# RWKV-7 recurrence in chunks, then hash-routed experts: score products in quarters, the old state by diagonal blocks, C in both layouts, and the decay exchange moved to TensorE

## The chip, the cores and the metric

The kernel runs on one core of one Trainium2 chip. The metric is the device time of one execution in microseconds (us), lower is better. One run gives one time; a separate profiled execution gives the trace.

## The reference

Four batches of eight heads, 768 steps, head size 40, all float32. The recurrence is sequential over the steps; its output, with all heads side by side (3072 rows of 320), goes through one of eight experts, chosen by a hash of the token's id.

```python
for t in range(S):                                   # S = 768
    y[:, :, t] = einsum('bhd,bhde->bhe', rt, state)  # state before the step
    Sa = einsum('bhde,bhe->bhd', state, at)
    state = state * wt[:, :, None, :] - einsum('bhd,bhe->bhde', Sa, bt) \
            + einsum('bhd,bhe->bhde', vt, kt)
x = y.transpose(0, 2, 1, 3).reshape(B * S, H * D)
expert = token_ids * 2654435761 % 8
out[expert == e] = maximum(x[expert == e] @ w1[e], 0) @ w2[e]   # (320, 1024), (1024, 320)
```

## The kernel before

**Chunks.** The steps are cut into 12 chunks of 64. A tile is one chunk of two batches, so there are 24 tiles, and two states (`st`, ring of `NG` = 2) that alternate. `u` is the tile's number, `C` = 64, `D` = 40, `R` = 104, `HP` = 4 pairs of heads; `par` tells the head of a pair, `be` the batch. The two heads of a pair lie at columns or partitions 0 to 39 and 64 to 103 (`half40`); 40 to 63 between them are zero. Within a chunk the recurrence becomes matrix products: decayed inputs are formed, a triangular system is inverted, and all steps of the chunk follow from it.

**The order.** Every step is put into `plan` with a tick by `at_tick(tick, step)`, where the tick's fraction is the step's place in `STEPS`. The list is then sorted, and TensorE, VectorE, ScalarE and GpSimd each take their instructions in exactly that order (`manual_schedule`); each waits for what it needs and holds up all that stands behind it. Only SyncE's queue (SP), which issues most loads, is ordered by the framework. One tick is one tile's worth: tile u has its first part at tick u, its second at tick u + `LAG` = u + 8. So ticks 0 to 7 hold first parts alone (the fill), 8 to 23 both, 24 to 31 second parts alone (the drain).

**First part** (`tile_a`). Loads of a, b, k and of the decay products p and q; GpSimd multiplies them to `at` (for a) and `z` (for b and k) at tick u - 0.3; TensorE turns both (`t_ps`, `z_ps`, an identity product each), ScalarE copies them to `at_t` and `z_t`. Step `a` makes the scores `a_ps`: 16 products (`quarters()`: pair, head, batch) of 40 partitions, 128 columns of `z_t` and 64 of `at_t`. Six ScalarE copies take out the diagonal blocks `pk` and the block `no` between them, and VectorE multiplies the rest with the mask `after` into `mk`, straight from PSUM.

**Inversion** (`group_i`). Four tiles at a time, VectorE transposes `pk` to `nb`, does 31 pairs of an outer product (L460) and an addition (L463), and transposes the result to `ut` and `ug`. GpSimd makes `um` from `ug`.

**Second part** (`tile_m`, `tile_s`, `tile_b`). `x_ps` and `u_ps` complete the inverse; `r_ps` is old state by `at_t` (step `r0`, in the tick before) plus `mk` by v (step `r1`); `c_ps` is that by `um`, C's transpose, which ScalarE copies into `x_t`. Step `nc` turns C back by eight transposes into `x`, with two ScalarE copies. Step `rc` makes the read-out scores `rc_ps` from `x_t` and `r_t` (16 products again), VectorE masks them to `mr`. Step `s` adds the old state, by an identity product of all 104 rows and 320 columns for each batch, and 16 products of `z` and `x`; VectorE scales by `pend` into `st`. Step `y` multiplies `r_t` with `sd` (the state turned, step `sd`) and `mr` with `z`; VectorE scales by `py` to `xs`, and two GpSimd DMAs write it to `x_rows`.

**Decay rounds** (`decays`). Six times, for four tiles each, VectorE forms running products of w over quarters of 32 steps (`pb`, `qb`), each step an instruction. The two halves of a chunk lie in different partitions, so the end product of one half is written to HBM and read back for the other (`end_dram`, `ends`). GpSimd scales p (L310) and q (L316) and issues their stores; rounds start five ticks ahead of need.

**Routing and experts.** The routing is cut into steps from tick 8 on, two a tick (`sums_ps` counts tokens; `mine` compares ids with an iota of GpSimd). Eight experts follow, each a gather, 24 + 32 products, and a scatter.

**PSUM.** All the attention's products use one pool of 4 buffers of two banks.

Of the kernel before, what the change touches and what calls it, by code (L numbers as in the profile page):

```python
# [41 lines left out]
def kernel(  # L42
# [74 lines left out]
    psa = apool("psa", 4, space=bass.MemoryType.PSUM)  # L117

# [33 lines left out]
    en_r = ring("en", 2, [BLK, HP, P], all_of)  # L152
# [16 lines left out]
    end_dram = [nc.dram_tensor(f"end{i}", (RN, 3, B * H, D), F32) for i in range(NR)]  # L169

    def psum(name):
        return psa.tile([P, 2, 512], F32, tag="psa", name=name)

    def bank(shape, name):
        n = 1
        for s in shape[1:]:
            n *= s
        t = psum(name)[:, 0, 0:n]
        return t if len(shape) == 2 else t.rearrange("p (x y) -> p x y", x=shape[1])
# [34 lines left out]
    STEPS = ["r1", "at_t", "z0", "c", "z1", "r_t", "nc", "rc", "a", "s", "x", "r0", "y", "v_t", "u", "sd"]  # L214
# [15 lines left out]
    def decays(ri, t0, span, t_ends):  # L230

        x = rounds[ri]
        todo = []

        def step(f):
            todo.append(f)
            return f
# [5 lines left out]
        BH = B * H  # L243

        def store(i, src):
            for y in range(2 * RN):
                nc.gpsimd.dma_start(pq_dram[ri][i][y * HC:(y + 1) * HC].rearrange("t bh e -> bh t e"),
                                    src[y * BH:(y + 1) * BH].rearrange("p (t e) -> p t e", e=D))

        def ends_rows(i):  # L250

            return end_dram[ri][:, i:i + 2].rearrange("n x bh e -> n (x bh) e")

        @step
        def _():
            x["pb"] = pb = work.tile([P, HC * D], F32, tag="pb", name="pb", bufs=1)
            x["qb"] = qb = work.tile([P, (HC + 1) * D], F32, tag="qb", name="qb", bufs=1)
# [3 lines left out]
            nc.sync.dma_start(end_dram[ri][:, 2], ones[0:RN * BH, 0:D])  # L261
# [5 lines left out]
        @step  # L267
        def _():
            nc.vector.memset(segs(x["pb"])[:, :, 0, :], 1.0)


        qs = [x_ for x_ in range(SL - 2, -1, -1)]
        for i in range(1, SL):
            @step
# [3 lines left out]
        for i in qs:  # L278
            @step
# [4 lines left out]
        @step  # L284
        def _():
# [3 lines left out]
            x["ends"] = ends = work.tile([P, SEG + 1, D], F32, tag="ends", name="ends", bufs=1)  # L289
# [6 lines left out]
        @step  # L296
        def _():
            ends = x["ends"]
            nc.vector.tensor_tensor(ends[:, 0:SEG], x["own"][:],
                                    ends[:, SEG].unsqueeze(1).to_broadcast([P, SEG, D]), op=OP.mult)  # L300
            nc.sync.dma_start(ends_rows(0), ends[:, 0])
# [4 lines left out]
        @step  # L306
# [6 lines left out]
        @step  # L313
        def _():
            q = segs(x["qb"])
            nc.gpsimd.tensor_tensor(q, q, x["ends"][:, 1:].unsqueeze(2).to_broadcast([P, SEG, SL, D]),  # L316
                                    op=OP.mult)
            nc.gpsimd.tensor_copy(x["qb"][:, HC * D:], x["ends"][:, SEG])
            store(1, x["qb"][:, D:])

        for i, f in enumerate(todo):
            at_tick(t0 + span * i / len(todo), order=8)(f)

        @at_tick(t_ends)
        def _():

            en = en_r(ri)
            for rn in range(RN):
                nc.sync.dma_start(en[rn * B:(rn + 1) * B].rearrange("b hp (two x) -> b (hp two) x", two=2)[:, :, 0:D],
                                  end_dram[ri][rn, 0].rearrange("(b h) e -> b h e", h=H))  # L330

        @at_tick(t_ends + 1.0)
        def _():
            en = en_r(ri)
            p = bank([P, HP, B * RN], "en_ps")
            for hp in range(HP):
                nc.tensor.transpose(p[0:R, hp, :], en[0:B * RN, hp, 0:R], ident[0:B * RN, 0:B * RN])
            x["pend"] = t = work.tile([P, HP, RN, B], F32, tag="pend", name="pend", bufs=NR)
            nc.scalar.copy(t[0:R].rearrange("p h n b -> p h (n b)"), p[0:R])
# [4 lines left out]
    def tile_a(u):  # L344
# [38 lines left out]
        for i in range(2):  # L383
            @at_tick(u, f"z{i}")
            def _(i=i):
                if i == 0:
                    x["z_t"] = work.tile([P, 2, HP, P], F32, tag="z_t", name="z_t", bufs=1)
                    x["z_ps"] = psum("z_ps")
                p = x["z_ps"][0:R, i, :].rearrange("p (h t) -> p h t", h=HP)
                for hp in range(HP):  # L390
                    nc.tensor.transpose(p[:, hp, :], x["z"][:, i, hp, :], ident[:])  # L391
                nc.scalar.copy(x["z_t"][0:R, i], p)
                if i == 1:
                    x.pop("z_ps")

        @at_tick(u, "a")
        def _():
            gi, ti = divmod(u, GRP)
            p = psum("a_ps")
# [20 lines left out]
            for be in range(2):  # L420
                rows = half(1 - be)
                nc.vector.tensor_tensor(mk[rows], scores(rows, be, 0, C),  # L422
                                        after[rows].unsqueeze(1).unsqueeze(1).to_broadcast([C, 2, HP, C]), op=OP.mult)
# [50 lines left out]
    def hx(p, hp):  # L474

        return p * HP + hp
# [32 lines left out]
    def tile_s(u, t0):  # L509
# [12 lines left out]
        @at_tick(t0 - 1.0)  # L522
# [11 lines left out]
        def _():  # L534

            x["x_t"] = t = work.tile([P, HP, 2 * P], F32, tag="x_t", name="x_t", bufs=1)
            p = psum("v_ps")
# [7 lines left out]
    def tile_b(u, t0):  # L545
# [6 lines left out]
        def _():  # L552
            x["r1_ps"] = p = psum("r1_ps")[:, 0, :]
# [18 lines left out]
        def _():  # L572
            p = psum("c_ps")
            for hp, par, be in quarters():
                rows = (half if par == 0 else half40)(par)
# [401 lines left out]
```

## Time and profile before

| | |
|---|---|
| median of 3 runs | 1059.66 us (1057.06 to 1066.82) |
| profiled execution | 1068.85 us, span 1067.0 us |
| mean granted TensorE clock | 0.851 |
| TensorE busy | 869.2 us, 81% |
| VectorE / ScalarE / GpSimd busy | 407.8 / 241.9 / 317.8 us |
| DMA | 83.26 MB, mean 78 GB/s |
| from the start to the first inner product of the second part (`x_ps`) | 161.75 us |
| first start of `rc_ps`, of tile 1 | 214 us |
| `rc_ps` of tile 1 to that of tile 16 (15 full ticks) | 357 us |
| `rc_ps` of tile 16 to that of tile 22 (6 drain ticks) | 98 us |
| from 686 us on: gather, experts, scatter | 381 us |

Times are counted from the first instruction. A matrix product stands in the trace as two records, a weight load (PEld) beside each; a transpose as one. [...] A busy TensorE is not TensorE at its peak; what tells is the distance from the start of one group to the start of the next. In the square brackets of a timeline stands how long the engine had been idle and what ended it.

### The profile page before, as it was taken

Reading aid. Unit: us, or ns where it says so; the run is one execution under the profiler, and the core shown is the slowest. Engines: PE = TensorE matmul, PEld = TensorE weight load, DVE = VectorE, ACT = ScalarE, POOL = GpSimd, SP = SyncE. Lnnn points to the kernel's source line nnn. Section 1 sums busy time; section 2 is a strip of 40 time slices with the busy share of each in tenths; the row PEclk is TensorE's granted clock in tenths of the full one; section 3 lists DMA queues with packets and bytes.
Section 4 is the critical chain, followed back from the end, with each engine's and each line's share of the span. In section 5 each row is a group of like instructions: output and inputs, shape, how many; then the busy total and the mean of one; then the engine's idle time right before and its main releaser. Section 6 shows DMA issues by size and latency. Waiting matters only on the chain.

```text
span 1067.0 us, 21146 instructions
## 1 busy us (share of the span) xinstructions
PE 869.2 (81%) x8886; PEld 622.3 (58%) x8886; DVE 407.8 (38%) x831; ACT 241.9 (23%) x544; POOL 317.8 (30%) x392
## 2 busy tenths in 40 slices
PE   0128275599899979999999999679999999999994
PEld 0027265488777868887887778525354453544533
DVE  6223797678765774334445721110110101101110
ACT  0014143233334333334333322100100000000000
POOL 3562523622553482322222112031120211201101
PEclk9999998687778866557666976679999999999997
DMA  3744553642454354332112221352241222312000
GB/s 71 159 98 103 111 113 64 137 99 62 97 104 94 64 104 89 67 67 48 30 30 39 52 39 24 111 165 68 75 140 56 88 69 77 136 62 69 19 1 21
DMA packets 164338, 83.26 MB, mean 78 GB/s; under 512 B 140942, under 2 KB 152975, under 8 KB 164240
## 3 DMA queue, kind: packets, MB, share of 16 engines
q1 hardware_dynamic: 154256, 56.95, 23.6%
q0 software_dynamic: 9984, 24.93, 9.5%
q8 instruction: 71, 1.16, 0.5%
q14 instruction: 27, 0.22, 0.1%
HBM read 65.76 MB, written 17.39 MB: 78 GB/s over the span
## 4 chain that ended last, share of the span: by engine, by line
PE 69%; DVE 8%; DMA 6%; ACT 5%; POOL 5%; issue 4%; SPq 3%; POOLq 0%; DVEq 0%; ACTq 0%
PE up_ps L821 18%; PE dn_ps L831 13%; PE s_ps L195 5%; PE a_ps L195 5%; PE rc_ps L195 5%; PE r_ps L195 4%; PE y_ps L195 4%; PE u_ps L195 2%; PE sd_ps L646 2%; PE z_ps L391 2%; PE t_ps L429 2%; PE nc_ps L588 2%; PE x_ps L195 1%; DMA ends<-end 1%; PE c_ps L195 1%
## 5 line engine op out<-in xcount | busy, mean ns | idle before, releaser
L821 PE MATMUL up_ps<-xt,w 128*128 128x512 f32 (+1 forms) x384 | 191.7, 630 | 8.6 <-issue 8.6
L821 PEld LDWEIGHTS up_ps<-xt,w 128*128 128x128 f32 (+1 forms) x384 | 62.7, 189 | 133.4 <-issue 133.4
L831 PE MATMUL dn_ps<-w,ht 128*128 128x320 f32 x512 | 139.9, 434 | 0.0
L831 PEld LDWEIGHTS dn_ps<-w,ht 128*128 128x128 f32 x512 | 96.6, 190 | 45.3 <-issue 6.1
L835 POOL DMA_INDIRECT out_dram<-o,idx_all x32 | 32.0, 999 | 272.0 <-ACT o L834 236.0
L638 POOL DMA_DIRECT2D x_rows<-xs x48 | 28.1, 590 | 268.5 <-DVE xs L635 142.4
L429 PE MATMUL t_ps<-ident,at 128*104 128x128 f32 x96 | 22.7, 380 | 81.8 <-POOL at L374 81.8
L824 DVE TENSOR_SCALAR ht<-up_ps 128x512 f32<-128x512 f32 x32 | 22.1, 692 | 174.6 <-PE up_ps L821 138.8
L463 DVE TENSOR_TENSOR ub<-ub,outer 128x31 f32<-128x31 f32 (+15 forms) x186 | 85.9, 462 | 6.4
L195 PE MATMUL a_ps<-at_t,z_t 40*128 40x64 f32 x768 | 84.8, 388 | 0.4
L460 DVE TENSOR_TENSOR outer<-ub,nb 128x31 f32<-128x31 f32 (+15 forms) x186 | 81.9, 440 | 3.9
L195 PEld LDWEIGHTS a_ps<-at_t,z_t 40*128 40x128 f32 x768 | 80.2, 296 | 4.5 <-issue 2.5
L599 DVE TENSOR_TENSOR mr<-rc_ps,after 128x1024 f32<-128x1024 f32 x24 | 29.3, 1222 | 125.0 <-PE rc_ps L195 125.0
L826 ACT ACTIVATE ht<-up_ps 128x512 f32<-128x512 f32 x32 | 19.1, 597 | 194.9 <-PE up_ps L821 194.9
L429 PEld LDWEIGHTS t_ps<-ident,at 128*104 128x104 f32 x96 | 13.9, 173 | 83.6 <-POOL at L374 82.2
L813 DVE COPY xt<-xg_ps 128x256 f32<-128x256 f32 x32 | 13.2, 412 | 128.2 <-PE xg_ps L811 128.2
L422 DVE TENSOR_TENSOR mk<-a_ps,after 64x512 f32<-64x512 f32 x48 | 33.1, 689 | 73.1 <-ACT no L417 72.6
L195 PE MATMUL rc_ps<-r_t,x_t 40*128 40x64 f32 x768 | 59.4, 313 | 0.8 <-ACT x_t L578 0.7
L195 PEld LDWEIGHTS rc_ps<-r_t,x_t 40*128 40x128 f32 x768 | 55.6, 220 | 4.5 <-ACT x_t L578 1.2
L391 PE MATMUL z_ps<-ident,z 128*104 128x128 f32 x192 | 41.8, 358 | 17.4 <-POOL z L376 7.8
L195 PE MATMUL s_ps<-st,ident 104*104 104x320 f32 x88 | 50.6, 726 | 0.0
L834 ACT COPY o<-dn_ps 128x320 f32<-128x320 f32 x32 | 13.6, 426 | 148.4 <-PE dn_ps L831 148.4
(148 smaller groups left out, 1275.4 us busy)
## 6 DMA issues: line engine op xcount, KB each, us to landing
w<-in_moe_w_dram SPq DMA_DIRECT2D x8, 1280.0 KB
w<-in_moe_w_dram SPq DMA_DIRECT2D x8, 1024.0 KB
ql<-q_rows SPq DMA_DIRECT2D x48, 160.0 KB
pb<-in_w_dram SPq DMA_DIRECT2D x24, 160.0 KB
al<-in_a_dram SPq DMA_DIRECT2D x48, 80.0 KB
kb<-in_b_dram SPq DMA_DIRECT2D x48, 80.0 KB
kb<-in_k_dram SPq DMA_DIRECT2D x48, 80.0 KB
r<-in_r_dram SPq DMA_DIRECT2D x48, 80.0 KB
```

Of the source, the lines that this page charges most:

```text
L195: nc.tensor.matmul(out_, lhsT=lhsT, rhs=rhs, start=start, stop=stop, skip_group_check=True)
L391: nc.tensor.transpose(p[:, hp, :], x["z"][:, i, hp, :], ident[:])
L422: nc.vector.tensor_tensor(mk[rows], scores(rows, be, 0, C), after[rows].unsqueeze(1).unsqueeze(1).to_broadcast([C, 2, HP, C]), op=OP.mult)
L429: nc.tensor.transpose(p[0:R, hp, :], src[:, hp, 0:R], ident[:])
L460: nc.vector.tensor_tensor(tv, ub[:, 0:j + 1, j:j + 1].to_broadcast([P, j + 1, m]), nb[:, j, j + 1:].unsqueeze(1).to_broadcast([P, j + 1, m ...
L463: nc.vector.tensor_tensor(o, o, tv, op=OP.add)
L599: nc.vector.tensor_tensor(t[:].rearrange("p two h t -> p (two h) t"), p[:].rearrange("p two (h t) -> p (two h) t", t=C), after[:].unsqueez ...
L638: nc.gpsimd.dma_start(x_rows[r0:r0 + C, :], xs[half(be), :])
L821: nc.tensor.matmul(p[:], lhsT=w1[0:m, c, f * P:(f + 1) * P], rhs=xt[0:m, c, 0:n], start=(c == 0), stop=(c == 2))
L824: nc.vector.tensor_scalar(ht[:, f, 0:n], p[:], 0.0, None, op0=OP.max)
L831: nc.tensor.matmul(p[:], lhsT=ht[:, f, j * P:(j + 1) * P], rhs=w2[:, f, :], start=(f == 0), stop=(f == FP - 1))
L835: st = nc.gpsimd.indirect_dma_start(out=out[:], out_offset=bass.IndirectOffsetOnAxis(ap=idx, axis=0), in_=o[:], in_offset=None, bounds_che ...
```

## The change

- **PSUM**: 4 buffers of one bank (`psa`, by `bank`) and 2 of two banks (`psb`, by `two_banks`), for z, a, v, c, rc and sd.
- **Scores**: each product of `a_ps` and `rc_ps` is made as two of 64 columns, in the order (half of the columns, head).
- **mk**: two ScalarE copies out of PSUM and one GpSimd product with `after`, in place of two VectorE products.
- **Old state**: four products of 40 columns of the identity with 160 columns of `st`, the two diagonal blocks alone; `st` scaled by two VectorE products of the blocks.
- **C**: `nc_ps` is 16 products of `um` and `r1` beside those of `c_ps`, in place of eight transposes of the copied C; C is copied to `x_t` in two halves.
- **Order**: new `STEPS`; `y` and `sd` at tick t0 + 1; py's load at t0; both z transposes and their copies in one step.
- **Decay rounds**: the end product of the first half goes to the second by a product with the matrix `partner` and an addition of `second`; no `end_dram`. q is scaled by VectorE; SP issues the stores; `pend` comes from one transpose. Rounds 0 and 1 both stand before tick -0.9; the load of a round has a step of its own one tick ahead.
- **Inversion**: its last step at +3.2 ticks, from +3.5.

```diff
-    STEPS = ["r1", "at_t", "z0", "c", "z1", "r_t", "nc", "rc", "a", "s", "x", "r0", "y", "v_t", "u", "sd"]
+    STEPS = ["r1", "at_t", "z", "c", "y", "r_t", "sd", "a", "rc", "x", "s", "v_t", "r0", "u"]
...
     def store(i, src):
             for y in range(2 * RN):
-                nc.gpsimd.dma_start(pq_dram[ri][i][y * HC:(y + 1) * HC]...
+                nc.sync.dma_start(pq_dram[ri][i][y * HC:(y + 1) * HC]...
...
-            nc.sync.dma_start(ends_rows(0), own[:, 0])
-            nc.sync.dma_start(ends[:, SEG], ends_rows(1))
+            p = bank([P, D], "f_ps")
+            nc.tensor.matmul(p, lhsT=partner[:], rhs=own[:, 0], start=True, stop=True)
...
+            nc.vector.tensor_scalar(ends[:, SEG], x.pop("f_ps"), second[:, 0:1], None, op0=OP.add)
...
-            nc.gpsimd.tensor_tensor(q, q, x["ends"][:, 1:].unsqueeze(2).to_broadcast([P, SEG, SL, D]),
+            nc.vector.tensor_tensor(q, q, x["ends"][:, 1:].unsqueeze(2).to_broadcast([P, SEG, SL, D]),
...
-            for hp, par, be in quarters():
-                c0 = (hp * 2 + be) * C
-                mm(p[:, par, c0:c0 + C], x["z_t"][half40(par), be, hp, :], x["at_t"][half40(par), hp, be, :])
+            for hp in range(HP):
+                for be in range(2):
+                    for i in range(2):
+                        for par in range(2):
+                            c0 = (hp * 2 + be) * C
+                            mm(p[half(i), par, c0:c0 + C], x["z_t"][half40(par), be, hp, half(i)],
+                               x["at_t"][half40(par), hp, be, :])
...
-                nc.vector.tensor_tensor(mk[rows], scores(rows, be, 0, C),
-                                        after[rows]...to_broadcast([C, 2, HP, C]), op=OP.mult)
+                nc.scalar.copy(mk[rows], scores(rows, be, 0, C))
+            mk = mk[:].rearrange("p two hp t -> p (two hp) t")
+            nc.gpsimd.tensor_tensor(mk, mk, after[:].unsqueeze(1).to_broadcast([P, H, C]), op=OP.mult)
...
+                q = bank([P, DM], "nc_ps")
+                for hp, par, be in quarters():
+                    c0 = (2 * hp + par) * D
+                    mm(q[half(be), c0:c0 + D], um[half(be), hx(par, hp), :], r1[half(be), hp, par * C:par * C + D])
...
                 for be in range(2):
-                    mm(p[0:R, be, 0:DM].rearrange("p (hp two e) -> p hp two e", hp=HP, two=2), ident[0:R, 0:R],
-                       heads(st[:, be]), stop=False)
+                    for par in range(2):
+                        cols = slice(par * C, par * C + D)
+                        mm(p[half40(par), be, :].rearrange("p (hp e) -> p hp e", hp=HP), ident[0:R, cols],
+                           st[:, be, :, cols], start=be == 0, stop=False)
...
-        @at_tick(t0, "y")
+        @at_tick(t0 + 1, "y")
...
-            @at_tick(t0, "sd")
+            @at_tick(t0 + 1, "sd")
...
-    for ri in range(NR):
-        decays(ri, max(ri * RN * NG - 5.0, -2.5 + ri), 0.8, max(ri * RN * NG - 2.0, 1.0 + ri))
+    decays(0, -3.0, 0.4, -2.5, 0.3)
+    decays(1, -1.7, 0.4, -1.2, 0.3)
+    for ri in range(2, NR):
+        t0 = ri * RN * NG - 5.0
+        decays(ri, t0, 0.7, t0 + 1.0, 0.3)
...
-        group_i(gi, t0 + 0.05, t0 + 0.1, t0 + 3.5)
+        group_i(gi, t0 + 0.05, t0 + 0.1, t0 + 3.2)
```

## Rows read from the trace of the kernel before

**Rows 1.** Busy time by stage: engines' us (instructions), granted clock, DMA share, GB/s

```profile
214.00:368.00 154.00, 141.40 (x2328) 120.67 (x2327) 107.16 (x218) 59.78 (x140) 58.94 (x71) 0.77 0.45 88
368.00:571.00 203.00, 188.23 (x2658) 163.15 (x2656) 96.81 (x194) 69.53 (x161) 79.20 (x98) 0.65 0.33 61
571.00:669.00 98.00, 90.68 (x1729) 76.98 (x1728) 37.05 (x79) 29.47 (x65) 18.79 (x31) 0.81 0.21 39
578.00:629.00 51.00, 45.92 (x1093) 39.39 (x1088) 29.96 (x68) 19.26 (x43) 12.58 (x21) 1.00 0.25 51
```

**Rows 2.** TensorE in order of time, a drain tick: start, us, line, operation

```profile
602.06 2.05 PE L195 MATMUL rc_ps<-r_t,x_t 40*128 40x64 f32 x32
604.04 1.32 PE L195 MATMUL s_ps<-st,ident 104*104 104x320 f32 x4
605.30 0.83 PE L195 MATMUL s_ps<-x,z 128*40 128x40 f32 x32
...
607.29 0.72 PE L195 MATMUL y_ps<-sd,r_t 104*64 104x80 f32 x16
...
608.86 0.43 PE L541 MATMUL v_ps<-ident,x 64*104 64x64 f32 x8
...
610.27 0.92 PE L646 MATMUL sd_ps<-ident,st 104*104 104x104 f32 x8
611.12 1.13 PE L195 MATMUL r_ps<-x,mk 64*64 64x40 f32 x32
612.86 0.68 PE L195 MATMUL c_ps<-um,r 64*64 64x64 f32 x32 [0.62 <-ACT r L569]
613.48 0.64 PE L429 MATMUL t_ps<-ident,r 128*104 128x128 f32 x4
...
615.92 2.05 PE L195 MATMUL rc_ps<-r_t,x_t 40*128 40x64 f32 x32
```

**Rows 3.** The same of another drain tick

```profile
630.00 3.73 PE L195 MATMUL rc_ps<-r_t,x_t 40*128 40x64 f32 x32
...
648.85 1.12 PE L195 MATMUL c_ps<-um,r 64*64 64x64 f32 x32 [0.62 <-ACT r L569]
649.90 1.09 PE L429 MATMUL t_ps<-ident,r 128*104 128x128 f32 x4
...
653.16 3.73 PE L195 MATMUL rc_ps<-r_t,x_t 40*128 40x64 f32 x32
656.82 2.46 PE L195 MATMUL s_ps<-st,ident 104*104 104x320 f32 x4
```

**Rows 4.** TensorE in order of time, in the fill

```profile
76.65 1.09 PE L429 MATMUL t_ps<-ident,at 128*104 128x128 f32 x4 [19.61 <-POOL at L374]
...
89.45 4.43 PE L195 MATMUL a_ps<-at_t,z_t 40*128 40x64 f32 x32
...
98.47 4.43 PE L195 MATMUL a_ps<-at_t,z_t 40*128 40x64 f32 x32
...
161.75 1.06 PE L195 MATMUL x_ps<-ut,no 32*32 32x32 f32 x32 [3.83 <-DVE ut L471]
...
197.51 0.98 PE L689 MATMUL sums_ps<-mine,ones 128*128 128x192 f32 x2 [19.32 <-DVE mine L683]
```

**Rows 5.** Who waited for whom, all of the span: us in total, times, longest

```profile
DVE ends L299 <- DMA ends<-end: 31.9, 6, 5.8
```

**Rows 6.** GpSimd and VectorE in order of time, round 2

```profile
117.73 2.88 POOL L310 TENSOR_TENSOR pb<-pb,rends 128x1280 f32<-128x1280 f32 x1 [23.21 <-DVE rends L304]
117.82 2.87 DVE L463 TENSOR_TENSOR ub<-ub,outer 128x60 f32<-128x60 f32 x1
```

**Rows 7.** Groups by line: count, busy us, mean ns, idle before and its releasers

```profile
L376 POOL TENSOR_TENSOR z<-kb,ql 128x320 f32<-128x320 f32 x48 | 43.5, 926 | 9.0 <-DMA ql<-q_rows 5.6 <-DMA kb<-in_k_dram 3.4
...
L496 POOL TENSOR_SCALAR um<-ug,first 128x256 f32<-128x256 f32 x24 | 23.9, 994 | 3.0 <-DVE ug L472 2.5
...
L415 ACT COPY pk<-a_ps 32x256 f32<-32x256 f32 x48 | 17.4, 363 | 103.7 <-PE a_ps L195 103.4
```

More of the change, by code (lines that the diff above doesn't have):

```diff
@@ L168, with two_banks @@
     pq_dram = [[nc.dram_tensor(f"{n}_rows{i}", (RN * C, B * H, D), F32) for n in "pq"] for i in range(NR)]
-    end_dram = [nc.dram_tensor(f"end{i}", (RN, 3, B * H, D), F32) for i in range(NR)]
-    def psum(name):
-        return psa.tile([P, 2, 512], F32, tag="psa", name=name)
+    BH = B * H
+    second = hold.tile([P, 1], F32, name="second")
+    nc.vector.memset(second[:], 1.0)
+    partner = hold.tile([P, P], F32, name="partner")
+    nc.vector.memset(partner[:], 0.0)
+    for rn in range(RN):
+        c0 = rn * 2 * BH
+        nc.vector.tensor_copy(partner[:, c0:c0 + BH], ident[:, c0 + BH:c0 + 2 * BH])
+        nc.vector.memset(second[c0:c0 + BH], 0.0)
+    def two_banks(name):
+        return psb.tile([P, 2, 512], F32, tag="psb", name=name)
     def bank(shape, name):
@@ L381, in _ @@
             turn(t, x["at"])
[L383 to L389, printed above, removed]
+        @at_tick(u, "z")
+        def _():
+            x["z_t"] = t = work.tile([P, 2, HP, P], F32, tag="z_t", name="z_t", bufs=1)
+            p = two_banks("z_ps")
+            for be in range(2):
                 for hp in range(HP):
[L391 to L394, printed above, removed]
+                    nc.tensor.transpose(p[0:R, be, hp * P:(hp + 1) * P], x["z"][:, be, hp, :], ident[:])
+            for be in range(2):
+                nc.scalar.copy(t[0:R, be].rearrange("p h t -> p (h t)"), p[0:R, be])
         @at_tick(u, "a")
@@ L586, in _ @@
+            cols = x["x_t"][:].rearrange("p h (b t) -> p h b t", b=4)[:, :, ::3, :].rearrange("p h b t -> p b h t")
+            for par in range(2):
+                nc.scalar.copy(cols[half40(par)], p[half40(par), :, 0:HP * C].rearrange("p b (h t) -> p b h t", h=HP))
+            if not last:
                 for be in range(2):
-                    for hp in range(HP):
-                        nc.tensor.transpose(p[:, be, hp * R:(hp + 1) * R], x["x_t"][0:R, hp, be * P:(be + 1) * P],
-                                            ident[0:R, 0:R])
@@ L590, in _ @@
-                    nc.scalar.copy(x["x"][half(be), be, :, 0:R], p[half(be), be, 0:HP * R].rearrange("p (h x) -> p h x", h=HP))
+                    nc.scalar.copy(x["x"][half(be), be].rearrange("p hp (two e) -> p (hp two) e", two=2)[:, :, 0:D],
+                                   q[half(be)].rearrange("p (h e) -> p h e", h=H))
         @at_tick(t0, "rc")
         def _():
-            p = psum("rc_ps")
-            for hp, par, be in quarters():
-                c0 = (hp * 2 + be) * C
-                mm(p[:, par, c0:c0 + C], x["x_t"][half40(par), hp, be * P:(be + 1) * P], x["r_t"][half40(par), hp, be, :])
+            p = two_banks("rc_ps")
@@ L598, in _ @@
+            for hp in range(HP):
+                for be in range(2):
+                    for i in range(2):
+                        for par in range(2):
+                            c0 = (hp * 2 + be) * C
+                            s0 = be * P + i * C
+                            mm(p[half(i), par, c0:c0 + C], x["x_t"][half40(par), hp, s0:s0 + C],
+                               x["r_t"][half40(par), hp, be, :])
             x["mr"] = t = work.tile([P, 2, HP * 2, C], F32, tag="mr", name="mr", bufs=1)
```

121 lines of the change are left out of this document (54 added, 67 removed).

## Prediction

> **What bounds the kernel now.** I read the stages first, then TensorE's order of time within one tick, then the waits. The experts' stage, 381 us from 686 us on, is not touched, so all that can move lies before it. In the table of stages [rows 1] TensorE is busy 92 to 93% in both middle stages, while VectorE falls from 107 of 154 us to 97 of 203 us: TensorE's own order sets the tick. Its granted clock there is 0.77 and 0.65, that is a mixture of 1.2 and 2.4 GHz. The same drain tick lasts 13.86 us at 2.4 GHz, from one start of the decayed read-out scores (`rc_ps`) to the next [rows 2], and 23.16 us at 1.2 GHz [rows 3]. Before 214 us it is different: TensorE idles 19.6 us before the transposes of tile 1, because GpSimd does a decay round ahead of them, and 19.3 us for the routing's `mine` [rows 4]. So three sums are made: the fill (to the scores of tile 1 at 214 us), 15 full ticks (214 to 571, 23.8 us each), 6 drain ticks (571 to 669, 16.3 each).
>
> **Score products in quarters.** Now 16 products stand as 32 records and take 602.06 to 604.04 = 1.98 us at 2.4 GHz, 3.66 at 1.2 [rows 2, 3]. The change makes 64 records of 64 columns that go through four quadrants in turn. No row has 40 partitions in that form; the nearest is `c_ps` (64 partitions, 64 columns, the same turn of quadrants): 32 records in 0.62 us, at 1.2 GHz 1.05 [rows 2, 3]. Twice that is 1.24 and 2.10, a gain of 0.74 and 1.56 for each of `rc_ps` and `a_ps`. The other bound is the pace of `r_ps`, two quadrants in turn, 32 records in 1.13 us: 2.26 us, a loss of 0.28. I take `c_ps`, since quadrants and sizes are alike.
>
> **Old state by diagonal blocks.** The two identity products (4 records of 320 columns) take 604.04 to 605.30 = 1.26 us [rows 2], 2.4 at 1.2 GHz [rows 3]. Four products of half the width, two for each half of the columns, lie between no overlap (no gain) and full overlap (half). The state products behind them alternate halves too and take 0.83 us for 32, 26 ns a record, where 40 columns one half after the other stand at 35 (`r_ps`) [rows 2], so I take half: 0.63 and 1.2.
>
> **C in both layouts.** Today C's evacuation, the transposes of r, then eight transposes with two evacuations between stand before the scores: 614.12 (end of `t_ps`) to 615.92 = 1.80 us at 2.4 GHz, and 649.90 + 1.09 to 653.16 = 2.17 at 1.2 [rows 2, 3]. In their place stand 32 records like those of `r_ps` with x: both halves of the rows into one bank, 1.13 us [rows 2], at 1.2 GHz 1.13 x 1.05 / 0.62 = 1.91. Gain 0.67 and 0.26. The products of c write each half of the rows to its own bank; those of `r_ps` write both into one and run at 35 ns a record where c runs at 19. [...]
>
> C's evacuation becomes two copies on ScalarE instead of one; y, r's transposes and sd now lie between c and the scores, over 3 us of TensorE (y alone 607.29 to 608.86 [rows 2]), and hide it. If y were not there, the second copy would stand on the path, some 0.6 us. y and sd move into the next tick and cost the same there; y's wait for the masked scores goes, and x_rows, xs and the load of py move with it. On GpSimd the two x_rows issues, which wait for xs, now stand ahead of mk in the next tick; y ends some 2 us before a does, so they are out by then. The wait for r before c (0.62 us [rows 2]) is filled in a full tick by the at and z transposes, and stays in the drain.
>
> **TensorE's sum.** Drain tick: 13.86 - 0.74 - 0.63 - 0.67 = 11.8 us at 2.4 GHz; 23.16 - 1.56 - 1.2 - 0.26 = 20.1 at 1.2. Full tick: less the filled 0.62, plus at and z transposes (three groups of four: by sd's eight, 610.27 to 611.12 in rows 2, 0.43 each at 2.4 GHz; 1.09 long at 1.2, its tail beside the next, 0.95 taken [rows 4]) and the new `a_ps`: 11.8 - 0.6 + 1.3 + 1.24 = 13.7, and 20.1 - 0.6 + 2.8 + 2.1 = 24.4.
>
> **The mask of mk moves, and that is the new wait.** VectorE's product out of PSUM becomes two ScalarE copies and one GpSimd product of 128x512. GpSimd's order has mk of tile u, then um, and only then at and z of tile u+1, which were ready early until now. So a leg arises from the end of a to the next z: ScalarE six copies at 0.363 [rows 7] and two twice as wide, at most 0.73 each, together 3.5; mk between 0.926 x 512/320 = 1.48 and 2.88 x 512/1280 = 1.15, taken as 1.3; um 0.99; at and z three at 0.93 [rows 6, 7]; handovers 0.8: 9.4 us. TensorE has for that time rc 1.24, s, x and r0 2.6 (with 605.30 to 607.29 of rows 2), v and u 1.4 (608.86 to 610.27), r1 1.13, at 0.5 = 6.9. So a full tick at 2.4 GHz is 13.7 + 2.5 = 16.2, taken as 16.3 us; at 1.2 GHz TensorE's 24.4 covers the leg.
>
> **VectorE** had 204 us in these 15 ticks, 13.6 each [rows 1]; mk leaves, q's scaling comes (by GpSimd's time for p at most 2.9 a round, one round in four ticks [rows 6]), the waits for the exchange leave (31.9 us in six rounds [rows 5]). It stays under 16.
>
> **A full tick** by the clock of today: 0.77 x 154 + 0.65 x 203 over 357 us is 0.70, so 0.40 of the time at 2.4 GHz. 1 / (0.40 / 16.3 + 0.60 / 24.4) = 20.4 us. 15 ticks: 306 against 357, **-51**. Drain with 0.62 at 2.4 GHz (0.81 [rows 1]): 1 / (0.62 / 11.8 + 0.38 / 20.1) = 14.0, six: 84 against 98, **-14**.
>
> **The fill.** Round 0 loses its 5.3 us exchange (31.9 / 6) and GpSimd's scaling of q (as long as p's 2.88 [rows 6]) with four DMA issues. But GpSimd's order now has round 1's p before at of tile 0, and round 1's load must wait for the one `pb` buffer, until round 0's stores on SP have read it. I leave tile 0's scores where they are (76.65 - 19.6 - 4.4 = 52.6), 8 us either way. In return tiles 1 and 5 no longer wait 19.6 us each. The interval of tiles grows, from 9.0 (89.45 to 98.47 [rows 4]), by the same leg without um: a 2.1, ScalarE 3.5, mk 1.3, at and z 2.8, last z transposes 0.5, its two copies 1.2, handovers 0.8 = 12.2. Tile 7's scores end at 52.6 + 7 x 12.2 + 2.1 + 2.9 (round 2's p) = 143, and x follows at 144 against 161.75, if VectorE has `ut` by then: group 0 starts at about 95 and needs some 40. From there to 214 were 52 us, 19.3 of them the wait for `mine`, whose iota now stands before the round on GpSimd and no stores with it: 33, so 177. **-37**, bounds -15 and -50. SP gets eight stores a round in place of seven exchange and ends transfers; loads queued behind a store wait for its scaling, under 3 us, with two buffers of prefetch ahead.
>
> **Sum.** -51 - 14 - 37 = -102 of the profiled execution's 1068.85 us (span 1067.0): 967. The median of the runs, 1059.66, stands at 0.9914 of it: **959 us**.
>
> **Rivals.** (1) The clock rises. For: from 578 to 629 us, in ticks without the a products, it is 1.00 for 51 us [rows 1], and a and rc get denser. Against: TensorE idles 2.5 us a tick before z. At 0.8 of the time at 2.4 GHz a tick is 17.5 (262), a drain tick 12.9 (77): 177 + 262 + 77 + 17 + 381 = 914 + 2, as median **908**.
> (2) The clock falls, to 0.1 of the time: 23.2 (349) and 18.8 (113): 177 + 349 + 113 + 17 + 381 + 2 = 1039, **1030**.
> (3) The quarters don't overlap four-wise (the change does not do what it says): 2.26 and 3.9 a score, twice a tick: 18.3 and 28 us, 23.1 in the mixture, 347, drain 91, fill 180: 1018, **1009**.
> (4) Slower: GpSimd's leg rules at either clock. Its place is at and z of tile u+1 behind mk of tile u; its price is that GpSimd's products and VectorE's hold each other up: a VectorE product of 128x60 took 2.87 us while GpSimd scaled p [rows 6]. If every GpSimd product took double, the leg is 9.4 + 5.1 = 14.5, at 1.2 GHz 2.5 over TensorE's 12, and TensorE, idle in each tick, stays at 1.2 GHz: tick 26.9 (404), fill interval 15 (fill 197), drain 121: 197 + 404 + 121 + 18 + 383 = 1123, **1113**. With that fill and drain it decides from a tick of 23.4 on (350 of the 686 us are left for 15). Against it: most GpSimd products of this trace keep 0.93 [rows 7] though VectorE works beside them. [...]
>
> **How the numbers follow.** Chances: forecast 0.52, (1) 0.22, (2) 0.12, (3) 0.09, (4) 0.05. The range reaches from (1) with the better fill bound, 896, to (2), 1030, and holds (3). A change under 1% (10.6 us, about what a measurement of this kernel can tell) is only the seam between (2) and (4). Faster 0.92, same 0.03, slower 0.05.
>
> **What would show it.** `rc_ps` and `a_ps` as 64 records in 1.2 to 1.3 us at 2.4 GHz; the old state in 0.6; no TensorE wait between c and rc; a TensorE wait before z whose releaser is GpSimd's z; tiles 1 to 7 of the fill 12 us apart; no 19 us gaps. Wrong would make it a clock far from 0.70 between the first and the last full tick, ScalarE's copies late enough to hold the two-bank buffers (six uses a tick of two), or a decay round that starts late behind SP's stores.

## The result, and the profile after

The changed kernel takes **924.26 us** (median of 4 runs, 921.35 to 939.83) beside 1058.36 for the kernel before in the same session: ratio **0.876**, interval 0.866 to 0.886. Ratios and intervals, here and in the experiments, leave out the executions that the record marks as slow (here 939.83), so a ratio of two medians can differ from them by up to a per cent. The forecast was 959, its range 896 to 1030. The profiled execution has a span of 919.6 us, 147 less than before.

| | before | forecast | after |
|---|---|---|---|
| start of `rc_ps` of tile 1 (the fill) | 214 us | 177 | 184.0 |
| 15 full ticks, one | 357 us, 23.8 | 306, 20.4 | 270.2, 18.0 |
| 6 drain ticks, one | 98 us, 16.3 | 84, 14.0 | 70.7, 11.8 |
| granted clock, full ticks / drain | 0.70 / 0.81 | same | 0.85 / 0.95 |

The last line of the table comes from the windows by stage of the changed kernel, to be read beside [rows 1] (engines' busy us, then granted clock, share of the DMA engines, GB/s):

```profile
184.00:454.10 270.10, 231.76 (x6302) 206.19 (x6292) 194.01 (x378) 153.34 (x348) 141.78 (x166) 0.85 0.59 102
454.10:525.00 70.90, 67.04 (x2065) 62.15 (x2067) 38.10 (x80) 31.94 (x72) 19.05 (x32) 0.95 0.29 55
```

The two clocks that the prediction prices as 2.4 and 1.2 GHz are granted clocks of 1.00 and 0.50: in the kernel before, the windows 602:616 and 630:653 around its two drain ticks [rows 2, 3] give these shares. No run shows the frequencies themselves; the ticks' own lengths, 13.86 and 23.16 us, are what its sums use.

A drain tick at a granted clock of 1.00 (window 465.5:476.8), TensorE in order of time, answers to [rows 2]:

```profile
465.53 1.16 PE L203 MATMUL rc_ps<-r_t,x_t 40*64 40x64 f32 x64
466.62 0.69 PE L203 MATMUL x_ps<-ut,no 32*32 32x32 f32 x32
467.24 0.74 PE L203 MATMUL s_ps<-st,ident 104*40 104x160 f32 x8
467.81 0.81 PE L203 MATMUL s_ps<-x,z 128*40 128x40 f32 x32
...
472.37 0.66 PE L203 MATMUL c_ps<-um,r 64*40 64x64 f32 x32 [0.57 <-issue]
472.82 1.12 PE L203 MATMUL nc_ps<-r,um 64*64 64x40 f32 x32
473.87 0.78 PE L203 MATMUL y_ps<-sd,r_t 104*64 104x80 f32 x16
...
475.97 0.88 PE L653 MATMUL sd_ps<-ident,st 104*104 104x104 f32 x8
476.78 0.93 PE L203 MATMUL rc_ps<-r_t,x_t 40*64 40x64 f32 x48
```

From start to start the scores take 1.09 us (forecast 1.24, before 1.98), the old state 0.57 (0.63, 1.26), C's second layout 1.05 (1.13), the whole tick 11.25 (11.8, 13.86). Between c and the next rc TensorE does not wait; the wait before c (0.57, forecast 0.62) stays.

In a full tick, the wait stands where the prediction put it: before the transposes of at and z, with GpSimd as releaser. TensorE and then GpSimd, the same stretch:

```profile
379.86 1.13 PE L203 MATMUL r_ps<-x,mk 64*64 64x40 f32 x32
382.16 0.64 PE L428 MATMUL t_ps<-ident,at 128*104 128x128 f32 x4 [1.17 <-POOL at L371]
382.98 1.93 PE L386 MATMUL z_ps<-ident,z 128*104 128x128 f32 x8 [0.18 <-POOL z L373]
```

```profile
377.72 1.28 POOL L422 TENSOR_TENSOR mk<-mk,after 128x512 f32<-128x512 f32 x1 [3.90 <-ACT mk L420]
379.17 1.06 POOL L759 DMA_INDIRECT slot_tokens<-token,key_i  x1 [0.17 <-issue]
380.28 0.99 POOL L495 TENSOR_SCALAR um<-ug,first 128x256 f32<-128x256 f32 x1
381.26 0.85 POOL L371 TENSOR_TENSOR at<-al,pl 128x320 f32<-128x320 f32 x1
382.07 1.69 POOL L373 TENSOR_TENSOR z<-kb,ql 128x320 f32<-128x320 f32 x2
```

The scores of this tick end at 374.24, z at 383.76: a leg of 9.5 us (forecast 9.4). A scatter of the routing (1.06) stands in it that the forecast had not counted; the handovers, ScalarE's copies and z were shorter by as much. TensorE waits 1.4 us of the forecast 2.5, because it begins with at while GpSimd still makes the second z. Nor does it wait in every tick: in the 15 full ticks at costs it 8.0 us in nine waits, z 2.3. Ticks of tiles 8 to 14 last 16.8 to 17.4 us each, with one stretch of 3.4 us at a clock of 0.50 that begins within 1.1 us of the start of the at transposes; before and behind it the clock is 1.00.

One wait of TensorE was in no forecast: the exchange product. The chain of waits, engine and line, what it waited for, us in total, times, longest:

```profile
PE f_ps L293 <- DVE own L291: 81.4, 6, 28.4
PE t_ps L428 <- POOL at L371: 48.5, 16, 6.2
```

Two of the six lie before the first tile (17.5 and 28.4 us). The other four are 8.25, 13.09, 6.96 and 7.20 us: 35.5 us. The second and the third of these, and the start of `x_ps` of tile 0:

```profile
142.88 0.69 PE L203 MATMUL x_ps<-ut,no 32*32 32x32 f32 x32
156.67 0.65 PE L293 MATMUL f_ps<-own,partner 128*128 128x40 f32 x2 [13.09 <-DVE own L291]
...
223.47 0.65 PE L293 MATMUL f_ps<-own,partner 128*128 128x40 f32 x2 [6.96 <-DVE own L291]
```

The two last of the four stand in the long full ticks, of 28.1 and 26.7 us. The exchange through HBM had cost VectorE 31.9 us of waiting [rows 5]; as a product, in the four rounds behind the first tile alone, TensorE waits 35.5 us, since it takes its instructions in order and this one waits for the whole round on VectorE.

### The profile page after: what moved, and what is told of

Its sections match the earlier page's. It is cut to its first block, busy times and chain, and to the rows that moved or that the text cites. A ratio compares the mean times of both kernels' runs of the same rounds, so it can differ in the third digit from the quotient of the medians.

```text
span 919.6 us, 25403 instructions
## 1 busy us (share of the span) xinstructions
PE 720.6 (78%) x11032; PEld 503.3 (55%) x11032; DVE 401.9 (44%) x807; ACT 281.5 (31%) x634; POOL 297.2 (32%) x354
## 3 DMA queue, kind: packets, MB, share of 16 engines
q8 instruction: 87, 1.43, 0.7%
## 4 chain that ended last, share of the span: by engine, by line
PE 59%; issue 8%; POOL 6%; DVE 5%; DMA 3%; SPq 2%; ACT 0%; POOLq 0%; DVEq 0%
PE up_ps L831 21%; PE dn_ps L841 15%; PE y_ps L203 4%; PE z_ps L386 2%; PE nc_ps L203 2%; PE r_ps L203 2%; PE c_ps L203 2%; PE s_ps L203 2%; PE rc_ps L203 1%; PE u_ps L203 1%; POOL z L373 1%; POOL um L495 1%; PE t_ps L428 1%; PE xg_ps L821 1%; POOL at L371 1%
## 5 line engine op out<-in xcount | busy, mean ns | idle before, releaser
L462 DVE TENSOR_TENSOR ub<-ub,outer 128x31 f32<-128x31 f32 (+15 forms) x186 | 92.3, 496 | 6.4
L422 POOL TENSOR_TENSOR mk<-mk,after 128x512 f32<-128x512 f32 x24 | 32.0, 1332 | 112.2 <-ACT mk L420 95.2
L293 PE MATMUL f_ps<-own,partner 128*128 128x40 f32 x12 | 3.9, 424 | 81.4 <-DVE own L291 81.4
L645 POOL DMA_DIRECT2D x_rows<-xs x48 | 25.9, 544 | 116.4 <-DVE xs L642 69.6
L844 ACT COPY o<-dn_ps 128x320 f32<-128x320 f32 x32 | 13.6, 426 | 148.4 <-PE dn_ps L841 148.4
L428 PE MATMUL t_ps<-ident,at 128*104 128x128 f32 x96 | 21.0, 358 | 48.5 <-POOL at L371 48.5
L293 PEld LDWEIGHTS f_ps<-own,partner 128*128 128x128 f32 x12 | 3.0, 310 | 82.2 <-DVE own L291 82.2
L386 PE MATMUL z_ps<-ident,z 128*104 128x128 f32 x192 | 44.5, 401 | 3.9 <-POOL z L373 3.9
L373 POOL TENSOR_TENSOR z<-kb,ql 128x320 f32<-128x320 f32 x48 | 44.3, 941 | 0.0
L816 POOL DMA_INDIRECT xg<-x_rows,src_all x32 | 30.9, 967 | 35.5 <-PE xg_ps L821 18.6
L311 POOL TENSOR_TENSOR pb<-pb,rends 128x1280 f32<-128x1280 f32 x6 | 19.6, 3272 | 63.8 <-DVE rends L305 63.8
L386 PEld LDWEIGHTS z_ps<-ident,z 128*104 128x104 f32 x192 | 31.9, 187 | 12.8 <-POOL z L373 11.5
```

Source lines behind the costliest of these rows:

```text
L373: nc.gpsimd.tensor_tensor(heads(x["z"][:, be]), view(x["kb"][:, be]), view(x["q"][:, be]), op=OP.mult)
L386: nc.tensor.transpose(p[0:R, be, hp * P:(hp + 1) * P], x["z"][:, be, hp, :], ident[:])
L422: nc.gpsimd.tensor_tensor(mk, mk, after[:].unsqueeze(1).to_broadcast([P, H, C]), op=OP.mult)
L428: nc.tensor.transpose(p[0:R, hp, :], src[:, hp, 0:R], ident[:])
L462: nc.vector.tensor_tensor(o, o, tv, op=OP.add)
L645: nc.gpsimd.dma_start(x_rows[r0:r0 + C, :], xs[half(be), :])
```

## Experiments

Every kernel ran beside runs of the kernel before; ratios with intervals are to those. Session 1 (the first four): before 1059.76; session 2 (the next four): 1064.12; session 3: 1080.36.

### 1. What raised the clock: wide scores again, and quarters alone

```diff
-            for hp in range(HP):
-                for be in range(2):
-                    for i in range(2):
-                        for par in range(2):
...
+            for hp, par, be in quarters():
+                c0 = (hp * 2 + be) * C
+                mm(p[:, par, c0:c0 + C], x["z_t"][half40(par), be, hp, :], x["at_t"][half40(par), hp, be, :])
```

(the same for `rc_ps`; the second kernel makes the reverse edit in the kernel before)

> The changed kernel with both score products as 16 of 128 columns again, all else as changed. Theory (the quarters themselves raise the granted clock in full ticks): the clock between the first and the sixteenth read-out scores falls from about 0.86 towards the 0.70 of the kernel before, a full tick goes from 18 to some 22.5 us, the time to about 1030. Rival (the clock rose because of the waits that left, whatever the scores): the clock stays above 0.82 and the scores cost only their own length, 0.87 us each at 2.4 GHz twice in a full tick, some 26 us there, 7 in the drain, about 17 in the fill at 1.2 GHz: 975.

> The kernel before with the quarter scores and nothing else of the change. Theory (quarters raise the clock): clock in full ticks from 0.70 to over 0.82, full tick from 23.8 to about 18, time about 955. Rival (they give only their own length): clock stays about 0.70, a full tick loses 2.6 us, a drain tick 1.1, the fill some 10: 1003.

Measured: wide scores in the changed kernel **967.3** (0.921, 0.905 to 0.937); quarters alone in the kernel before **976.8** (0.931, 0.911 to 0.951). The 15 full ticks of each, first the wide scores, then the quarters alone:

```profile
198.20:491.20 293.00, 275.84 (x5368) 253.42 (x5366) 197.71 (x379) 152.94 (x348) 140.64 (x166) 0.76 0.54 94
```

```profile
208.10:501.40 293.30, 245.82 (x5941) 211.48 (x5940) 206.10 (x411) 129.15 (x300) 136.55 (x169) 0.85 0.46 89
```

The clock goes from 0.70 to 0.85 by the quarters alone, though TensorE's waits in the full ticks are no shorter than in the kernel before (11.2 us for C's copies, before 11.1; 17.9 for `mr`, before 3.1), and from 0.85 to 0.76 when they are taken out of the change. Each figure is of one profile; a second one of the changed kernel has 0.81 there. The first theory has the direction; taking them out did not bring back 0.70, so the rest of the change raises it too (0.76), and the two do not add. In time the same: the ratios give 7% by quarters alone, 8% by all else, 12% by both. Neither pair of expected times was met: 967 lies nearest to the rival's 975, and 977 between 955 and 1003. That the quarters raise the clock is shown; why they do is not.

### 2. The GpSimd leg: at and z ahead of mk, and mk back on VectorE

```diff
-        @at_tick(u - 1.0)
+        @at_tick(u - 1.6)
...
-        @at_tick(u - 0.3)
+        @at_tick(u - 0.55)
```

> The changed kernel with GpSimd's at and z of tile u+1 ahead of mk of tile u (tick u+0.45 instead of u+0.7), and the tile's loads 0.6 ticks earlier. Theory (the new GpSimd leg sets 2.1 us of idle TensorE in each full tick, and the clock falls behind that idle time): no TensorE wait for at or z, ticks 8 to 15 from 17.0 to 13.5 to 15.0 us, tiles of the fill 9 to 10 us apart instead of 12, time 850 to 885. Rival (the wait only moves, to um or to ScalarE's copies of r): ticks stay within 1 us of 17.0, time 910 to 925.

```diff
-                nc.scalar.copy(mk[rows], scores(rows, be, 0, C))
-            mk = mk[:].rearrange("p two hp t -> p (two hp) t")
-            nc.gpsimd.tensor_tensor(mk, mk, after[:].unsqueeze(1).to_broadcast([P, H, C]), op=OP.mult)
+                nc.vector.tensor_tensor(mk[rows], scores(rows, be, 0, C), after[rows]...to_broadcast([C, 2, HP, C]), op=OP.mult)
```

> The changed kernel with mk made by VectorE straight from the scores in PSUM again (two products of 0.69 us), no copies of mk on ScalarE, no product on GpSimd. Theory (the leg over ScalarE's copies and GpSimd's mk is what TensorE waits for ahead of at): the wait before the at transposes and the stretch at 1.2 GHz behind it go, ticks 8 to 15 from 17.0 to 14.0 to 15.0 us, tiles of the fill about 10 us apart instead of 12, time 885 to 900. Rival (VectorE's order holds the product behind the steps of the inversion, a_ps keeps its two-bank buffer longer, and sd or c waits instead): ticks 16.5 to 18, time 918 to 935.

Measured: at and z first **913.1** (0.871, 0.858 to 0.883), mk on VectorE **916.9** (0.868, 0.859 to 0.878). Both take the wait out of the full ticks: in all of the span TensorE's waits for at fall from 48.5 us in 16 to 20.3 in 5 and 21.8 in 6, and single ticks of 13.6 to 14.7 us appear. But both intervals overlap that of the changed kernel (0.866 to 0.886). Yet ticks 8 to 14 average 16.8 with at first and 15.9 with mk on VectorE, against 17.1. With at first, something else takes the place. From its TensorE in order of time:

```profile
333.72 0.31 PE L203 MATMUL x_ps<-ut,no 32*32 32x32 f32 x8
336.80 0.85 PE L203 MATMUL x_ps<-ut,no 32*32 32x32 f32 x24 [2.76 <-issue]
```

This is a gap in the middle of one group of products, with no releaser; for the next 14 us products take as long as at a clock of 0.50 (`r_ps` with mk 1.93 us, 1.13 in the tick before). More on the gaps stands in the last section. So the leg was there with its forecast length, but the time behind it was not free to be taken: the first theory's 850 to 885 fell, and of the rival only the time and the mean tick were right. With mk on VectorE the ticks lie between the two expectations, the time at the rival's edge: `a_ps` waits for its buffer behind mk 7.7 us in 3, and the gaps are 12.0 us.

### 3. The exchange product later, and the rounds moved

The first kernel moves the product of rounds 2 to 5; the second also gives `pb` two buffers and puts round 1 behind tile 0's first part.

```diff
-            p = bank([P, D], "f_ps")
-            nc.tensor.matmul(p, lhsT=partner[:], rhs=own[:, 0], start=True, stop=True)
-            x["f_ps"] = p
...
+        @then.append
+        def _():
+            p = bank([P, D], "f_ps")
+            nc.tensor.matmul(p, lhsT=partner[:], rhs=x["own"][:, 0], start=True, stop=True)
+            x["f_ps"] = p
...
-        decays(ri, t0, 0.7, t0 + 1.0, 0.3)
+        decays(ri, t0, 0.7, t0 + 1.5, 0.3)
```

```diff
-        @at_tick(t0 - 1.0)
+        @at_tick(-3.5 if ri == 1 else t0 - 1.0)
...
-            x["pb"] = pb = work.tile([P, HC * D], F32, tag="pb", name="pb", bufs=1)
+            x["pb"] = pb = work.tile([P, HC * D], F32, tag="pb", name="pb", bufs=2)
...
-    decays(1, -1.7, 0.4, -1.2, 0.3)
+    decays(1, -0.25, 0.9, 0.9, 0.3)
```

> The changed kernel with the exchange product of decay rounds 2 to 5 half a tick behind VectorE's last product (t0 + 1.5 instead of t0 + 0.7) and what follows it half a tick later. Theory (VectorE does the whole round in one piece in its order, and the new state, hence r0, stands behind it; the exchange product is only where TensorE shows the wait): the two long full ticks of 28 and 27 us fall by at most 4 us each, TensorE's wait moves to r_ps with releaser st; time 912 to 924. Rival (the exchange's place in TensorE's order costs it all): the two ticks fall to 18 and the fill loses some 10 more, time 890 to 900.

> The changed kernel with the decay rounds moved only: two buffers for pb, round 1 behind tile 0's first part (its products from tick -0.25 on), the exchange product of rounds 1 to 5 half a tick or more behind VectorE's last product. Theory (the exchange product in TensorE's order and round 1 ahead of tile 0 cost the fill): tile 0's scores start at 40 to 46 us instead of 58.9, TensorE's waits for own fall from 81 us to under 25, read-out scores of tile 1 at 165 instead of 184, the long ticks as with the later exchange: time 895 to 905. Rival (VectorE's own work, some 125 us of it before the first read-out scores, bounds the fill): they start within 5 us of 184, time 912 to 920.

Measured: later **916.9** (0.869, 0.841 to 0.898), rounds moved **910.4** (901.3, 903.7, 917.1 and 920.1, for which the record has no ratio). With the product later, TensorE's waits for own are those of rounds 0 and 1 alone:

```profile
PE t_ps L428 <- POOL at L371: 62.6, 17, 7.3
PE f_ps L296 <- DVE own L291: 42.9, 2, 28.1
```

The 28.1 and 26.7 us ticks become 15.1 and 17.0, and the ticks behind them 23.0 and 22.9; in the first of these GpSimd scales p ahead of at, and TensorE waits 5.33 us for at. No wait of r0 for st shows: the mechanism of the first theory of this kernel is wrong, though its time (912 to 924) was met, and the rival has the place right. The four ticks from each long one on took 83.3 and 77.8 us and now take 73.4 and 73.6; the 890 to 900 of the rival is not reached.

With the rounds moved, tile 0's scores start at 39.0 us in place of 58.9 and the read-out scores of tile 1 at 167.6 in place of 184.0; the waits for own are 15.8 us. That is the first theory's mechanism, and near its size in the fill (40 to 46 and 165 were expected); of the four times two lie in its 895 to 905. TensorE's longest wait is then 18.9 us for at of tile 0, in place of the 28.4 for own.

### 4. C's second layout in two banks

```diff
-                q = bank([P, DM], "nc_ps")
+                q = two_banks("nc_ps")
...
-                    mm(q[half(be), c0:c0 + D], um[half(be), hx(par, hp), :], r1[half(be), hp, par * C:par * C + D])
+                    mm(q[half(be), be, c0:c0 + D], um[half(be), hx(par, hp), :], r1[half(be), hp, par * C:par * C + D])
```

> The changed kernel with C's second layout in two banks, one for each half of the rows, all else as changed. The 32 records take 1.06 us at 2.4 GHz as changed, those of c_ps 0.47. Theory (two halves of the rows that write one bank run one after the other): they fall to about 0.5, a drain tick from 11.3 to 10.8, time about 912. Rival (they use only two of the four quadrants, since rows and columns change together, and that sets 33 ns a record): unchanged length, time 921 to 930, the upper end if nc now waits for a two-bank buffer.

Measured: **934.4** (0.883, 0.876 to 0.891). A drain tick's products:

```profile
484.39 1.12 PE L203 MATMUL nc_ps<-r,um 64*64 64x40 f32 x32
485.45 0.77 PE L203 MATMUL y_ps<-sd,r_t 104*64 104x80 f32 x16
```

1.06 us, as in one bank. The time is over both expectations; nc now waits for its two-bank buffer, 6.4 us in 11. So the first theory is wrong: that both halves of the rows write one bank does not set this pace, and the price by the row (1.13) is within 0.07 us of both. The two-quadrant rival is what is left of the two: `c_ps` uses four quadrants in turn and takes 0.45. That it is the quadrants is argued, not shown: `c_ps` differs from `nc_ps` in its operands too (64x40 and 64 columns, against 64x64 and 40).

### 5. y and sd in their own tick

```diff
-    STEPS = ["r1", "at_t", "z", "c", "y", "r_t", "sd", "a", "rc", "x", "s", "v_t", "r0", "u"]
+    STEPS = ["r1", "at_t", "z", "c", "r_t", "a", "rc", "x", "s", "v_t", "r0", "y", "u", "sd"]
...
-        @at_tick(t0 + 1, "y")
+        @at_tick(t0, "y")
...
-            @at_tick(t0 + 1, "sd")
+            @at_tick(t0, "sd")
```

(py's load goes back to t0 - 1)

> The changed kernel with y and sd back in their own tick (behind r0 and u), so that only r's transposes, and a in a full tick, lie between C and the read-out scores. Theory (y and sd hide C's two ScalarE copies): TensorE waits for x_t ahead of rc, 0.8 to 1.2 us a drain tick (11.3 to about 12.3), in a full tick 0.5 or less since a lies between; time 930 to 945. Rival (C's copies are short beside r's transposes and a): no wait ahead of rc, time within 6 us of the changed kernel's.

Measured: **956.2** (0.887, 0.878 to 0.896), beside 930.1 for the changed kernel in the same session, and over both expectations. But not by the theory's wait. A drain tick's transposes of r and the scores behind them, and a line of the waits:

```profile
505.72 0.64 PE L428 MATMUL t_ps<-ident,r 128*104 128x128 f32 x4
506.30 0.92 PE L203 MATMUL rc_ps<-r_t,x_t 40*64 40x64 f32 x46
```

```profile
PE sd_ps L653 <- DVE st L625: 15.3, 6, 3.0
```

TensorE goes from r's transposes straight to the scores; the drain tick is 11.3 us, not 12.3, and in all of the span the products of rc wait for `x_t` 1.0 us, in 2 places. What y's later place saves is in other ticks: the 15 full ones take 301.2 us here (270.2 and 281.4 in two profiles of the changed kernel). In the changed kernel sd does not wait for the new state behind VectorE (15.3 us here), and the gaps without a releaser are shorter (23.1 us here, 11.2 and 13.5 in those two); that these two make up the difference is not shown.

### 6. All orders together, with fewer loads, with other stores

The fourth kernel of session 2 (all orders) joins the rounds moved with at and z first, and gives the four load tiles three buffers. The next two are built on it: one leaves out the loads of a, b and k from tile 3 on and uses the values of three tiles before, the other lets ScalarE issue the decay stores, behind `pend`'s copies.

```diff
-            load(lambda be, rows: by_head(al[rows]), a, 2 * g, n * C)
+            if u >= 3:
+                x["a"], x["kb"] = tiles[u - 3]["a"], tiles[u - 3]["kb"]
+                return
...
```

```diff
-                nc.sync.dma_start(pq_dram[ri][i][y * HC:(y + 1) * HC]...
+                nc.scalar.dma_start(pq_dram[ri][i][y * HC:(y + 1) * HC]...
```

> The rounds moved, and at and z ahead of mk, with three buffers for the loads of a tile (earlier by 0.6 ticks). Theory (the three waits are separate and add): ticks of 14.2 us where no instruction gap falls in, fill some 25 us shorter, time 870 to 890. Rival (a denser TensorE order meets more of the gaps without a releaser that stand at every 256th record, and loads and VectorE take the place of the waits): 900 to 915.

> As all orders together, but from tile 3 on a, b and k are not loaded: the values of three tiles before are used again (work left out: 126 loads of 64 x 8 rows of 160 bytes... 64,500 of 208,000 packets). Theory (the gaps without a releaser at every 256th TensorE record are instruction loads that stand behind the kernel's own transfers, and the clock falls behind them): the gaps fall from 21 us to under 8, the clock between the read-out scores of tiles 1 and 16 rises from 0.84 to over 0.90, full ticks from 16.6 to about 14.5 us, the fill loses its waits for al and kb (some 20 us), time 840 to 860. Rival (the gaps don't depend on the transfers): they stay above 18 us, only the fill gains, time 880 to 890.

> All orders together, and the stores of a decay round issued by ScalarE behind pend's copies instead of SP. Theory (SP's queue holds a tile's loads behind stores that wait for p and q: at waits some 10 us for al twice in the fill): these two waits fall under 5 us each, tiles of the fill closer together, time 885 to 897. Rival (the transfers themselves, 0.66 of the engines' time in the fill, are what at waits for, or ScalarE's issues hold its copies): no gain, time 898 to 910.

> The changed kernel as it is, beside the others on one chip: 915 to 930.

Measured: all orders **902.0** (0.849, 0.842 to 0.857), loads left out **887.1** (0.828, 0.819 to 0.836), stores on ScalarE **934.5** (0.869, 0.863 to 0.875), the changed kernel again **930.1** (0.865, 0.857 to 0.872).

The changed kernel's two ratios, 0.876 and 0.865, lie 1% apart: the single orders of experiments 2 and 3, 0.868 to 0.871, can't be told from it. All orders has the lowest median of those that do all the work, some 2 to 3% ahead of the changed kernel by the ratios; but two of the four times with the rounds moved alone (901.3 and 903.7) are as low, so what at and z first adds is not shown. Its rival holds: the gaps are 20.9 us in 17 (11.2 in 14 as changed), and in the fill at waits for its loads, 10.78 and 9.42 us in two places. With the loads left out the DMA engines' share in the full ticks is 0.46 instead of 0.64, the clock there 0.89 (over 0.90 expected) and the gaps 13.6 us: neither under 8, nor above 18; the time is the rival's. With stores on ScalarE all the transfers are there and the gaps are 14.0 us. So that transfers make the gaps, or make them longer, is not shown. Stores on ScalarE hold its copies: TensorE waits 42.8 us for `z_t` (longest 20.1), and the time is over both expectations.

## Why the prediction was right, and where its size was off

**The sum of TensorE's parts held**: scores, old state and C each within 0.2 us, the drain tick at a clock of 1.00 within 0.6 (11.25 for 11.8). The full tick's sum without waits, 13.7, is borne out where at and z first takes the wait away. From one rc to the next, 13.62 us, at the pace of a clock of 1.00 (rc 1.11, transposes of at 0.65), with one wait of 0.56 us, of v for ScalarE:

```profile
389.03 1.11 PE L203 MATMUL rc_ps<-r_t,x_t 40*64 40x64 f32 x64
...
395.81 0.65 PE L428 MATMUL t_ps<-ident,at 128*104 128x128 f32 x4
...
402.65 0.53 PE L203 MATMUL rc_ps<-r_t,x_t 40*64 40x64 f32 x24
```

The leg over ScalarE and GpSimd held too (9.5 for 9.4), and so did the place of TensorE's wait before at and z and VectorE's slack (194 us busy in 270).

**The clock is the term that was mis-sized.** "A full tick by the clock of today" took 0.40 of the time at a clock of 1.00, as before, and 0.62 in the drain. Measured are 0.85 and 0.95, that is 0.70 and 0.90 of the time. With these shares and the prediction's own two ticks, 1 / (0.70 / 16.3 + 0.30 / 24.4) = 18.1 us, against 18.0 measured; the drain 1 / (0.90 / 11.8 + 0.10 / 20.1) = 12.3, against 11.8. By these two, 15 x 18.1 and 6 x 12.3, the ticks would have been forecast at 345 us in place of 390: 45 of the 49 us to the measured 341. That 18.1 comes so near is in part luck. The 16.3 us hold 2.6 us of wait in every tick at a clock of 1.00; in all 15 ticks, at and z cost 10.3 us. Beside them stand 14.2 us for the exchange product and 10.9 us of the gaps that the last section describes, which were in no sum. Rival (1) had the direction; with 0.8 of the time at a clock of 1.00 it came to 908, 16 us under, where the forecast is 35 over. That a and rc are what raises it, the first two experiments bear out: quarters alone take the clock from 0.70 to 0.85.

**The fill** came out at 184.0 for 177. Tile 0's scores started at 58.9, not 52.6, inside the 8 us either way: VectorE's round 1 stands 14.5 us, until 38.93, for what the profile puts down to a transfer, and TensorE and GpSimd's at behind it; with two buffers and round 1 later the scores start at 39.0.

```profile
38.93 0.83 DVE L264 TENSOR_SCALAR qb<-pb 128x1280 f32<-128x1280 f32 x1 [14.47 <-DMA ql<-q_rows]
```

From there the tiles stood 11.8 us apart (forecast 12.2), and x began at 142.9 (144). Behind it came the wait that was not in the sum, 13.09 us for the exchange product. The prediction wrote that "the waits for the exchange leave"; they changed engines. The step that was moved to TensorE waits there for its input from VectorE (35.5 us in the last four rounds), with all of TensorE's order behind it.

**Of C's evacuation** the statement that y hides its second copy, and that it costs some 0.6 us otherwise, fell: without y there the scores of the tick shown start at once, and over all ticks their products wait 1.0 us for `x_t`.

**The other rivals**: a falling clock is excluded by 0.85 and 0.95; quarters that don't overlap four-wise are excluded by 1.09 us; GpSimd's leg at doubled price by its 1.28, 0.99, 0.85 and 0.85 us (z: 1.69 for two).

## What to carry to other kernels

When a change splits TensorE's products over more quadrants, price each tick at both clock levels as here (1.00 and 0.50), but do not carry over the old share of each, which went from 0.40 to 0.70 at 1.00 here: let the forecast and its rivals be the shares. When a step moves to an engine with a fixed order, its waiting can move with it (here 31.9 us on VectorE before, 35.5 on TensorE after): look up what its input waits for, at the place in that order, and put it where that input is long done. And before a wait is taken out, look at what else in the same tick ends at nearly the same time: here two ways of removing the leg gave at most 1%, where 3 to 8 were expected.

## What the runs showed of the hardware

**TensorE's gaps without a releaser.** The idle times named "issue" inside a group of the attention's products lie for the most part, in all kernels with quarters, at the same place of the count of TensorE's records (matmuls, weight loads and the semaphore and branch instructions between them): number 256 n + 193. Others lie elsewhere, up to four in a kernel, most under 0.5 us (the longest 1.76, with quarters alone); what ends these stays open. Counted from the traces, gaps over 0.25 us at these places, from 100 us on:

```
kernel               records  gaps  sum us  longest
before                 17999     0     0
wide scores again      19227     0     0
quarters alone         21071     4     5.2     1.86
changed                22299    14    11.2     1.44
changed, again         22299    13    13.5     1.95
mk on VectorE          22321    13    12.0     1.83
at and z first         22316    17    22.4     3.04
exchange later         22303    12    15.5     3.02
rounds moved           22303    12    13.6     2.20
nc in two banks        22309    14    15.2     3.06
all orders             22321    17    20.9     3.05
all, loads left out    22321    14    13.6     2.00
all, ScalarE stores    22320    13    14.0     2.44
y in own tick          22285    18    23.1     2.82
```

The page of the changed kernel has a queue that fits (packets, MB, share of the engines):

```profile
q8 instruction: 87, 1.43, 0.7%
```

22299 records are 87.1 times 256, and 1.43 MB in 87 are 16.4 KB each; before it was 71, with 17999 records, 70.3 times 256. In the changed kernel's trace each of these gaps over 0.5 us ends 1.2 to 1.5 us after such a packet has landed. One in the changed kernel:

```profile
278.64 1.12 PE L203 MATMUL rc_ps<-r_t,x_t 40*64 40x64 f32 x64
279.70 0.50 PE L203 MATMUL x_ps<-ut,no 32*32 32x32 f32 x19
281.01 0.38 PE L203 MATMUL x_ps<-ut,no 32*32 32x32 f32 x13 [0.81 <-issue]
```

Its packet went from 278.83 to 279.79. `a_ps` and `rc_ps` together are 256 records, and run in some 2.1 us. That a packet brings TensorE its next 256 instructions, and that a gap is TensorE waiting for them, is the author's estimate from these counts and times; no run shows it. The longest gap of all orders together, 3.05 us before 256.02, had its packet from 253.58 to 254.55, which set out 3.1 us after the record 256 before the gap's had begun; in the gap of 281.01 that was 0.9 us. What makes the long ones long stays open: with a third of the kernel's packets gone the gaps were 13.6 us, with all of them 14.0 (stores on ScalarE) and 20.9, and the changed kernel alone gave 11.2 and 13.5. So quarters came with a price of their own, which the forecast did not know: more records for the same columns (17999 to 21071 by the quarters alone, 19227 to 22299 beside the rest of the change), and gaps of 5.2 and 11.2 us where the wide scores have none.
